# Chunked attention and a gated feed-forward layer on one core: steps of blocks 2 to 4 moved, the weights' sign by a sloped ReLU, and more products on nothing in block 0's attention

## The chip, the cores and the metric

The kernel runs on one core of one Trainium2 chip. The core has five engines that run side by side and each take their instructions in order: TensorE (PE in the profile; its weight loads are PEld), VectorE (DVE), ScalarE (ACT), GpSimd (POOL) and SyncE (SP), which here issues the transfers. The metric is the device time of one execution in microseconds (us).

## The reference

Queries, keys and values have 8 batches, 8 heads, 576 positions and 64 columns. Attention works within chunks of 64 positions, and its output goes through a feed-forward layer with a gate:

```python
scores = scale * np.matmul(q_c, k_c.transpose(0, 1, 2, 4, 3))
scores = scores - np.max(scores, axis=-1, keepdims=True)
attn = np.exp(scores)
attn = attn / (np.sum(attn, axis=-1, keepdims=True) + 1e-09)
out = np.matmul(attn, v_c)
...
h = x @ w_in                        # x: 4608 x 512, w_in: 512 x 2048
relu6 = np.clip(h + 3.0, 0.0, 6.0)
g = h * relu6 / 6.0
return (g @ w_out).astype(np.float32)   # w_out: 2048 x 512
```

All is in 32-bit floats.

## The kernel before

**Tiles and blocks.** The 4608 rows of x are nine blocks of 512 tokens. A block's attention has two halves, dp = 0 and 1, of four heads each; (2, 1) below is the second half of block 2. The 2048 columns between the two products are 16 tiles, ft = 0 to 15. Each factor of a product is split into a high part that the array takes exactly and a low rest, and a product is three matmuls (`passes`, L221 to L223: high by high, high by low, low by high).

**Attention** (L128 to L209) goes in steps: `load_qk` and `load_v` (transfers, one tile each, so a load waits for the use before), `scores` (64 small matmuls, L154, into the PSUM tile "two"), `soft` steps 0 to 3 (row maximum m, L161; subtraction and exponential, L164 and L165; sums z with the reciprocal, L168 to L170; normalization, L172), `transpose` (eight on TensorE, L183, and ScalarE's copy back over e, L185), `values` (64 small matmuls, L194, and ScalarE's copy of the result as x, L203 or L200; for blocks 0 to 2 VectorE makes the low rest of x, L206, at the end of the slot). After block 0 there is one PSUM tile "two" for all of it.

**The weights** arrive as 64-bit floats, and `convert` (L100 to L116) makes the split 32-bit ones: ScalarE copies the high word with a scale (L106), VectorE shifts it left by three bits (L107), which pushes the sign out, and puts the sign back by an AND with the word and an OR (L108). Then ScalarE scales the low word (L110), VectorE adds it (L111), ScalarE makes the high part (L115) and VectorE the low one (L116). `convert` runs once for each of the 16 tiles, four of them for block 0's first products, the others behind `issue_after` bounds on block 1's softmax.

**The start.** Block 0's attention stands ahead of all products (L291 to L307). `warm_up(n)` issues n matmuls of the identity by itself into a tile that nobody reads, "products on nothing"; `WARM2` holds how many of them stand at five places: after both scores, after both softmaxes (36), none, and in each half's turn between transposes and values (6) and after the values (4).

**Slots.** Blocks 0, 1 and 2 are computed directly, in the order of `SEGMENTS`: block 0 with tiles 0 to 3, block 1 with 0 to 15, block 0 with 4 to 15, block 2 with 0 to 15. Each tile has two slots: in the even one `mm1` makes 12 matmuls into h, followed by the gate (ScalarE L233, VectorE L234, ScalarE L235, and VectorE L236 at the slot's end); in the odd one `mm2` makes 12 matmuls of an earlier tile's g (LAG tiles behind) into four accumulators, which are evicted after a segment's last tile (L259 to L266). At the end of each slot the steps that `plan` has for it are issued, by rank and then in the order in which they were put there. Ahead of slot 30 (`SUMS`) a scheduler of the framework may change the order on the engines; from there on the text's order stands (`manual_schedule`). So what is issued first on a queue keeps back what is behind it. The attention of blocks 2 to 4 is put at the slots 30, 38, 52, 60, 68 and 76 for (2,0), (2,1), (3,0), (4,0), (4,1) and (3,1), with the offsets of the list `later`; all six are even.

**Units.** Blocks 3 to 8 are later multiplied in pairs by seven products in place of eight, and need sums of weights. `prepare(m, p)` (L328 to L356) makes them in 16 units, which start at the slots 30, 33, 36, 40, 43, 46, 50, 53, 57, 60, 63, 67, 70, 73, 77 and 80. A unit has three steps in three slots in a row, of rank 20 (behind all attention steps of the slot): first three transfers of plain weights to DRAM (L333) and two adds of high and low parts on VectorE (L337); second four sums on VectorE (L347) and ScalarE's copy of their high parts into the tile hl (L350); third VectorE's low parts into hl (L352) and four transfers of hl to DRAM (L355). The tiles a and hl have one buffer each, so L350 waits until the unit before has sent its hl.

**After.** At slot 86 (`FREE`) the memory of the weights and units is given to the paired products: `fetch` loads the sums from DRAM, and `x_operands` makes the operands of blocks 3 and 4 (L372, L373) in the slots behind 86. Block 2's products end at slot 96 and the pending ones behind it; from there the paired products run to the end, with the attention of blocks 5 to 8 among them.

Of the kernel before, what the change touches and what calls it, by code (L numbers as in the profile page):

```python
# [8 lines left out]
F32 = mybir.dt.float32  # L9
# [4 lines left out]
AF = mybir.ActivationFunctionType  # L14
ALU = mybir.AluOpType
# [15 lines left out]
NFP = NFT // 2  # L31
# [2 lines left out]
SLOTS = 7 * NFP  # L34
HALF = [slice(0, CH), slice(CH, P)]
WARM = 11
WARM2 = (0, 36, 0, 6, 4)
LAG = 2


# [1 line left out]
def tile_kernel(ctx: ExitStack, tc: tile.TileContext, qk_in, v_in, weights, out):  # L42
    nc = tc.nc
    PE, ACT, DVE, POOL = nc.tensor, nc.scalar, nc.vector, nc.gpsimd
# [31 lines left out]
    def warm_up(n, a=some, b=some):  # L76
        if not n:
            return
        idle = ps_h.tile([P, NT], F32, name="h")[:, :b.shape[-1]]
        for _ in range(n):  # L80
            PE.matmul(idle, lhsT=a[:, :P], rhs=b, start=True, stop=True)
# [7 lines left out]
    words, w, w_h, w_l = {}, {}, {}, {}  # L89
    loaded = converted = 0  # L90

    def load_to(ft):
        nonlocal loaded
        while loaded < min(ft, NFT):
            t = w_tile(loaded, I32).rearrange("p l m t -> p (l m t)")
            nc.sync.dma_start(out=t.rearrange("p (m t) -> p m t", m=2), in_=weights[loaded].bitcast(I32).rearrange("m p t -> p m t"))
            words[loaded] = t.rearrange("p (n t) -> p n t", t=2)
            loaded += 1

    def convert(ft):  # L100

        u = wsc.tile([P, 1024], I32, name="u")
        r = wsc.tile([P, 1024], I32, name="r")
        lo, hi = words[ft][:, :, 0], words[ft][:, :, 1]

        ACT.activation(out=u.bitcast(F32), in_=hi.bitcast(F32), func=AF.Copy, scale=2.0 ** -112)  # L106
        DVE.tensor_scalar(out=u, in0=u, scalar1=3, scalar2=None, op0=ALU.logical_shift_left)  # L107
        DVE.scalar_tensor_tensor(out=u, in0=hi, scalar=-2 ** 31, in1=u, op0=ALU.bitwise_and, op1=ALU.bitwise_or)  # L108

        ACT.activation(out=r, in_=lo.bitcast(U32), func=AF.Copy, scale=2.0 ** -29)  # L110
        DVE.tensor_tensor(out=u, in0=u, in1=r, op=ALU.add)  # L111
        a = u.bitcast(F32).rearrange("p (m t) -> p m t", m=2)
        w[ft] = w_tile(ft, F32R)
        w_h[ft], w_l[ft] = w[ft][:, 0], w[ft][:, 1]
        ACT.copy(out=w_h[ft], in_=a)  # L115
        DVE.tensor_tensor(out=w_l[ft], in0=a, in1=w_h[ft].bitcast(F32), op=ALU.subtract)  # L116

    def convert_to(ft):
        nonlocal converted
        load_to(ft + 3)  # L120
        while converted < min(ft, NFT):
            convert(converted)
            converted += 1

    def two_banks(p):
        return p.tile([P, 2, NT], F32, name="two")
# [88 lines left out]
    def finish():  # L215
        while low:
            low.pop(0)()
# [56 lines left out]
    def moe_slots(n, ft, *seg):  # L274

        g = mm1(n, ft)
        yield
        pending.append((n, ft, g, *seg))
        if len(pending) > LAG:
            mm2(*pending.pop(0))  # L280
        yield
# [9 lines left out]
    with tc.tile_pool(name="ps_b", bufs=2, space=bass.MemoryType.PSUM) as ps_b:  # L291
        both = [Attention(0, dp, lambda: two_banks(ps_b)) for dp in range(NDP)]
        both[0].load()
        both[1].load(xp.tile([P, 2, NB, 2 * CH], F32, name="x"), gp.tile([P, 2, NB // 2, 2 * CH], F32, name="g"))
        load_to(4)
        for a in both:
            a.scores()
        warm_up(WARM2[0])
        both[0].softmax()
        both[1].softmax(gp.tile([P, 2, NB, CH], F32, name="g"))  # L300
        warm_up(WARM2[1])
        for a in both:
            a.transpose()
            warm_up(WARM2[3])
            a.values()
            finish()
            warm_up(WARM2[4])  # L307
    ps_o = pool("ps_o", 4, space=bass.MemoryType.PSUM)
    convert_to(2)

# [6 lines left out]
    def kept(m, p, i):  # L317

        if m:
            return stream_b[i, p // 4][:, p % 4]  # L320
        k = ORDER_A.index(i)
        return stream_a[p, k // 4][:, k % 4]

    def quarter(m, row, col):

        return (col, row) if m else (row, col)

    def prepare(m, p):  # L328
        cols = lambda k: slice(256 * k, 256 * k + 256)
        for i, row, col in ((1, 0, 0), (2, 0, 1), (4, 1, 1)):  # L330
            f, k = quarter(m, row, col)
            to = kept(m, p, i).rearrange("p (l t) -> p l t", l=2)
            nc.sync.dma_start(out=to, in_=w[p + NFP * f][:, :, m, cols(k)].bitcast(F32))  # L333
        a = sp.tile([P, 2, 512], F32, name="a")
        for f in range(2):
            h, l = [w[p + NFP * f][:, k, m].bitcast(F32) for k in range(2)]
            DVE.tensor_tensor(out=a[:, f], in0=h, in1=l, op=ALU.add)  # L337
        yield

        def q(row, col):  # L340
            f, k = quarter(m, row, col)
            return a[:, f, cols(k)]


        for to, x, y, op in ((q(1, 1), q(1, 0), q(1, 1), ALU.add), (q(1, 0), q(0, 0), q(1, 0), ALU.subtract),
                             (q(0, 0), q(1, 1), q(0, 0), ALU.subtract), (q(0, 1), q(0, 1), q(0, 0), ALU.subtract)):
            DVE.tensor_tensor(out=to, in0=x, in1=y, op=op)  # L347
        hl = sp.tile([P, 2, 2, 2, 256], F32R, name="hl")
        s = a.rearrange("p f (k t) -> p f k t", k=2)
        ACT.copy(out=hl[:, :, :, 0], in_=s)  # L350
        yield
        DVE.tensor_tensor(out=hl[:, :, :, 1], in0=s, in1=hl[:, :, :, 0].bitcast(F32), op=ALU.subtract)  # L352
        for i, row, col in ((5, 1, 1), (7, 1, 0), (6, 0, 0), (3, 0, 1)):
            f, k = quarter(m, row, col)
            nc.sync.dma_start(out=kept(m, p, i), in_=hl[:, f, k].rearrange("p l t -> p (l t)").bitcast(F32))  # L355
        yield  # L356


# [21 lines left out]
    def x_operands(s, eng):  # L380
# [6 lines left out]
        for i in ORDER_A:  # L387
# [6 lines left out]
            elif i == 6:  # L394
# [6 lines left out]

    plan = {}
    early = [(0, "load_qk"), (1, "load_v"), (2, "scores"), (2, "softmax"), (7, "transpose"), (10, "values")]
    later = [(-2, "load_qk"), (3, "load_v"), (3, "scores"), (4, "soft", 0), (4, "soft", 1), (5, "soft", 2), (5, "soft", 3),
             (8, "transpose"), (9, "values")]

    def put(n, dp, at, steps, stretch=1.0):
        a = Attention(n, dp)
# [7 lines left out]
    SUMS = first[1] + 22  # L416
    FREE = first[3] + 2 * (NFP + LAG + 1)
    for (n, dp), at in zip(((2, 0), (2, 1), (3, 0), (4, 0), (4, 1), (3, 1)), (30, 38, 52, 60, 68, 76)):
        put(n, dp, at, later)
    for u in range(2 * NFP):  # L420
        for k in range(3):
            plan.setdefault(SUMS + u * (FREE - 2 - SUMS) // (2 * NFP) + k, []).append((20, lambda: next(prep)))
    prep = (step for p in range(NFP) for m in range(2) for step in prepare(m, p))
    slot = 0
    sp = made = None
    order = ExitStack()

    for i, (n, lo, hi) in enumerate(SEGMENTS):
        last = all(m != n for m, *_ in SEGMENTS[i + 1:])
        for ft in range(lo, hi):  # L430
            if i == 0:
                convert_to(min(ft + 2, 4))
            elif slot < SUMS:

                with tc.issue_after(second.done.ins):
                    convert_to(5)
                with tc.issue_after(second.last.ins):
                    convert_to(min(6 + 2 * ft, NFT))
            elif slot == SUMS:
                scratch.close()  # L440
                sums = ExitStack()
                sp = sums.enter_context(tc.tile_pool(name="sp", bufs=1, side="right"))
                op = sums.enter_context(tc.tile_pool(name="op", bufs=4, side="right"))
                order.enter_context(tc.manual_schedule())
            for _ in moe_slots(n, ft, ft == lo, ft == hi - 1, not last):
                for _, f in sorted(plan.pop(slot, []), key=lambda s: s[0]):
                    f()
                finish()
                slot += 1
                if slot == FREE:  # L450
                    assert next(prep, None) is None
                    sums.close()
                    op = None
                    start.close()
                    upper.close()
                    xop_pool = pool("xop", 8, side="right")
                    wsp = pool("wsp", 3, side="right")
                    for _ in range(3):
                        fetch()
                    made = x_operands(0, DVE)  # L460
                elif slot > FREE:
                    next(made, None)
# [197 lines left out]
```

## Time and profile before

| | us |
|---|---|
| median of 3 runs (854.91 to 855.72) | 855.14 |
| the profiled execution | 855.06 |
| its span, first to last instruction | 853.1 |
| TensorE busy | 814.5 |
| VectorE busy | 635.8 |
| ScalarE busy | 369.1 |
| GpSimd busy | 132.0 |

How to read it: busy times are sums over the span and overlap each other. A timeline row gives start, length, engine, line, operation, what is written from what, and in brackets how long the engine had been idle and what ended it; several instructions alike in a row are one row with their count. A row of a windows table gives a stretch, its length, the busy time of TensorE, its weight loads, VectorE, ScalarE and GpSimd with the number of instructions, then the clock granted to TensorE (1.00 is full), the busy share of the transfer engines and GB/s. Matmuls overlap, so the length of one is more than the distance to the next.

### The profile page before, as it was taken

How to read it: one execution, taken by the hardware profiler on the slowest of the kernel's cores; microseconds unless marked ns; L12 is line 12 of the kernel's file. 1: busy time of each engine (PE TensorE's matmuls, PEld its weight loads, DVE VectorE, ACT ScalarE, POOL GpSimd, SP SyncE). 2: the span in 40 equal slices, each digit the busy share in tenths (PEclk: the TensorE clock that was granted, in tenths of full speed). 3: DMA queues.
4: the chain of work that ended last, by engine and by line, in shares of the span. 5: the costliest groups of instructions: out<-in, count | busy, mean ns of one | idle time of the engine just before them, and what ended most of it. 6: DMA issues, size and time to landing. Idle time of an engine off the chain costs nothing.

```text
span 853.1 us, 13690 instructions
## 1 busy us (share of the span) xinstructions
PE 814.5 (95%) x5683; PEld 658.7 (77%) x5683; DVE 635.8 (75%) x768; ACT 369.1 (43%) x455; POOL 132.0 (15%) x77
## 2 busy tenths in 40 slices
PE   7889999789998999999999999999999999999998
PEld 5766878568776777878878888788788887887886
DVE  5978997585866776487699946876899466669951
ACT  4747763243334334334455443344554333336330
POOL 0000000000001000022227002222370022326200
PEclk9898999899999999999999999999999999999999
DMA  9893003856768745166655576666554765555563
GB/s 365 315 360 120 13 0 112 247 184 214 220 187 296 237 160 196 60 232 226 244 189 191 229 254 228 233 214 245 204 192 167 234 226 178 207 186 197 197 212 134
DMA packets 50014, 172.86 MB, mean 203 GB/s; under 512 B 4640, under 2 KB 16928, under 8 KB 39200
## 3 DMA queue, kind: packets, MB, share of 16 engines
q1 hardware_dynamic: 49952, 171.99, 58.0%
q8 instruction: 45, 0.74, 0.3%
q14 instruction: 17, 0.14, 0.1%
HBM read 133.17 MB, written 38.80 MB: 202 GB/s over the span
## 4 chain that ended last, share of the span: by engine, by line
PE 67%; DVE 22%; ACT 5%; issue 3%; DMA 2%; POOL 0%; SPq 0%; ACTq 0%; DVEq 0%
PE acc L221 14%; PE acc L223 14%; PE acc L222 14%; PE h L221 7%; PE h L222 7%; PE h L223 7%; PE two L194 2%; DVE xop L373 2%; DVE m L161 2%; DVE r L234 2%; DVE z L168 1%; DMA w<-w_in_out 1%; DVE a L347 1%; DVE e L164 1%; DVE g L496 1%
## 5 line engine op out<-in xcount | busy, mean ns | idle before, releaser
L221 PE MATMUL acc<-xop,ws 128*128 128x512 f32 x528 | 208.6, 396 | 4.4 <-DVE u L484 4.4
L222 PE MATMUL acc<-xop,ws 128*128 128x512 f32 x528 | 205.8, 390 | 0.0
L223 PE MATMUL acc<-xop,ws 128*128 128x512 f32 x528 | 205.4, 390 | 0.0
L221 PEld LDWEIGHTS acc<-xop,ws 128*128 128x128 f32 x528 | 99.1, 188 | 27.6 <-DVE u L484 6.8
L373 DVE TENSOR_TENSOR xop<-g,xop 128x1024 fp32r<-128x1024 f32 x72 | 103.4, 1468 | 21.5 <-ACT xop L372 21.5
L223 PEld LDWEIGHTS acc<-xop,ws 128*128 128x128 f32 x528 | 99.1, 188 | 20.9
L222 PEld LDWEIGHTS acc<-xop,ws 128*128 128x128 f32 x528 | 99.2, 188 | 19.8
L372 ACT CAST xop<-g 128x1024 fp32r<-128x1024 f32 x72 | 74.4, 1051 | 78.9 <-PE acc L223 51.3
L504 POOL TENSOR_TENSOR g<-g 128x512 f32<-128x512 f32 x24 | 34.8, 1449 | 307.3 <-DVE g L496 307.3
L221 PE MATMUL h<-x,w 128*128 128x512 f32 x192 | 80.0, 419 | 2.1 <-ACT x L203 1.2
L222 PE MATMUL h<-x,w 128*128 128x512 f32 x192 | 78.4, 409 | 0.0
L223 PE MATMUL h<-x,w 128*128 128x512 f32 x192 | 77.8, 405 | 0.0
L222 PE MATMUL acc<-g,w 128*128 128x512 f32 x192 | 75.5, 393 | 0.3 <-DVE g L236 0.3
L221 PE MATMUL acc<-g,w 128*128 128x512 f32 x192 | 75.4, 397 | 0.1
L223 PE MATMUL acc<-g,w 128*128 128x512 f32 x192 | 75.4, 393 | 0.0
L234 DVE SCALAR_TENSOR_TENSOR r<-r,h 128x512 f32<-128x512 f32 x48 | 32.8, 683 | 50.7 <-ACT r L233 50.7
L495 ACT ACTIVATE r<-acc,half 128x512 f32<-128x512 f32 x72 | 48.5, 685 | 26.3 <-DVE acc L484 25.4
L495 ACT ACTIVATE r<-h,half 128x512 f32<-128x512 f32 x24 | 16.5, 687 | 95.0 <-DVE h L484 95.0
L222 PE MATMUL h<-xop,ws 128*128 128x512 f32 x144 | 56.2, 390 | 0.2 <-DVE xop L373 0.2
L221 PE MATMUL h<-xop,ws 128*128 128x512 f32 x144 | 56.3, 391 | 0.0
L223 PE MATMUL h<-xop,ws 128*128 128x512 f32 x144 | 56.1, 389 | 0.0
L496 DVE SCALAR_TENSOR_TENSOR g<-r,acc 128x512 f32<-128x512 f32 x72 | 48.6, 683 | 7.0 <-ACT r L495 6.7
(93 smaller groups left out, 1270.5 us busy)
## 6 DMA issues: line engine op xcount, KB each, us to landing
ws<-b SPq DMA_DIRECT2D x42, 1024.0 KB, 4.8
ws<-a SPq DMA_DIRECT2D x24, 1024.0 KB, 4.9
ws<-a SPq DMA_DIRECT2D x24, 768.0 KB, 4.3
qk<-qk_in SPq DMA_DIRECT2D x17, 1024.0 KB, 6.6
w<-w_in_out SPq DMA_DIRECT2D x16, 1024.0 KB, 13.4
v<-v_in SPq DMA_DIRECT2D x17, 512.0 KB, 5.1
a<-hl SPq DMA_DIRECT2D x32, 256.0 KB, 3.4
b<-hl SPq DMA_DIRECT2D x32, 256.0 KB, 3.4
```

The costliest lines, as they stand in the source:

```text
L161: DVE.tensor_reduce(out=self.m, in_=flat(self.s), axis=AX.X, op=ALU.max)
L164: DVE.tensor_tensor(out=flat(self.e), in0=flat(self.s), in1=wide(self.m), op=ALU.subtract)
L194: PE.matmul(po[o, s, a, i, :], lhsT=self.v[rows, a, i, o], rhs=self.aT[rows, a, i, o], start=True, stop=True)
L221: PE.matmul(ps, lhsT=a_h, rhs=b_h, start=first, stop=False, skip_group_check=more)
L222: PE.matmul(ps, lhsT=a_h, rhs=b_l, start=False, stop=False, skip_group_check=more)
L223: PE.matmul(ps, lhsT=a_l, rhs=b_h, start=False, stop=last, skip_group_check=more)
L234: DVE.scalar_tensor_tensor(out=r, in0=r, scalar=1.0, in1=h, op0=ALU.min, op1=ALU.mult)
L372: ACT.copy(out=t[:, :, 0], in_=src)
L373: DVE.tensor_tensor(out=t[:, :, 1], in0=src, in1=t[:, :, 0].bitcast(F32), op=ALU.subtract)
L495: return (lambda: ACT.activation(out=r, in_=ps, func=AF.Relu, bias=half, scale=1.0 / 6.0), lambda: DVE.scalar_tensor_tensor(out=out, in0=r ...
L496: lambda: DVE.scalar_tensor_tensor(out=out, in0=r, scalar=1.0, in1=ps, op0=ALU.min, op1=ALU.mult))
L504: sub = lambda o, x, y: lambda: POOL.tensor_tensor(out=o, in0=x, in1=y, op=ALU.subtract)
```

## The change

Three things change. (1) `WARM2` has 46, 12 and 18 for 36, 6 and 4, and the last count is issued behind the first half only: 88 products on nothing instead of 56. (2) In `convert` the first step is ScalarE's sloped ReLU: it scales by 2^-112, and negative inputs by 2^32 more, which sets a bit of the exponent that the shift by three then moves into the sign's place; VectorE's L108 is gone. (3) The steps in `later` are moved, most of them by one slot ahead, with `load_v` behind the first softmax steps; a unit of `prepare` has four steps in four slots (the two adds; the four sums; the copy into hl; the low parts and all seven transfers, those of hl first and those of plain weights behind them), and each unit is a generator of its own, so that one unit's last step can share a slot with the next one's first.

```diff
-WARM2 = (0, 36, 0, 6, 4)
+WARM2 = (0, 46, 0, 12, 18)
...
-        ACT.activation(out=u.bitcast(F32), in_=hi.bitcast(F32), func=AF.Copy, scale=2.0 ** -112)
+        ACT.activation(out=u.bitcast(F32), in_=hi.bitcast(F32), func=AF.Prelu, scale=2.0 ** -112, alpha=2.0 ** 32)
         DVE.tensor_scalar(out=u, in0=u, scalar1=3, scalar2=None, op0=ALU.logical_shift_left)
-        DVE.scalar_tensor_tensor(out=u, in0=hi, scalar=-2 ** 31, in1=u, op0=ALU.bitwise_and, op1=ALU.bitwise_or)
...
             finish()
-            warm_up(WARM2[4])
+            if a is both[0]:
+                warm_up(WARM2[4])
...
     def prepare(m, p):
         cols = lambda k: slice(256 * k, 256 * k + 256)
-        for i, row, col in ((1, 0, 0), (2, 0, 1), (4, 1, 1)):
-            f, k = quarter(m, row, col)
-            to = kept(m, p, i).rearrange("p (l t) -> p l t", l=2)
-            nc.sync.dma_start(out=to, in_=w[p + NFP * f][:, :, m, cols(k)].bitcast(F32))
         a = sp.tile([P, 2, 512], F32, name="a")
...
             DVE.tensor_tensor(out=to, in0=x, in1=y, op=op)
+        yield
         hl = sp.tile([P, 2, 2, 2, 256], F32R, name="hl")
...
             nc.sync.dma_start(out=kept(m, p, i), in_=hl[:, f, k].rearrange("p l t -> p (l t)").bitcast(F32))
+        for i, row, col in ((1, 0, 0), (2, 0, 1), (4, 1, 1)):
+            f, k = quarter(m, row, col)
+            to = kept(m, p, i).rearrange("p (l t) -> p l t", l=2)
+            nc.sync.dma_start(out=to, in_=w[p + NFP * f][:, :, m, cols(k)].bitcast(F32))
         yield
...
-    later = [(-2, "load_qk"), (3, "load_v"), (3, "scores"), (4, "soft", 0), (4, "soft", 1), (5, "soft", 2), (5, "soft", 3),
-             (8, "transpose"), (9, "values")]
+    later = [(-3, "load_qk"), (2, "scores"), (3, "soft", 0), (3, "soft", 1), (3, "load_v"), (4, "soft", 2), (4, "soft", 3),
+             (7, "transpose"), (8, "values")]
...
     for u in range(2 * NFP):
-        for k in range(3):
-            plan.setdefault(SUMS + u * (FREE - 2 - SUMS) // (2 * NFP) + k, []).append((20, lambda: next(prep)))
-    prep = (step for p in range(NFP) for m in range(2) for step in prepare(m, p))
+        unit = prepare(u % 2, u // 2)
+        for k in range(4):
+            plan.setdefault(SUMS + u * (FREE - 2 - SUMS) // (2 * NFP) + k, []).append((20, lambda unit=unit: next(unit)))
```

More of the change, by code (lines that the diff above doesn't have):

```diff
@@ L450, in tile_kernel @@
                 if slot == FREE:
-                    assert next(prep, None) is None
                     sums.close()
```

## The prediction

> **What bounds the kernel now.** I read the page first, then the windows of each stage, then the waits of TensorE by place, and only there the timelines.
>
> ```profile
> span 853.1 us, 13690 instructions
> ...
> PE 814.5 (95%) x5683; PEld 658.7 (77%) x5683; DVE 635.8 (75%) x768; ACT 369.1 (43%) x455; POOL 132.0 (15%) x77
> ```
>
> TensorE is busy for 95% of the span, so the time is TensorE's work plus the places where it idles or runs at a lower clock. The profiled execution took 855.06 us, 1.96 us more than its span, and stands 0.08 us under the median of 855.14 us; I sum against 855.06. The windows by stage (stretch, its length, then busy time of TensorE, weight loads, VectorE, ScalarE, GpSimd, then the granted clock) show where it idles:
>
> ```profile
> 0.00:23.30 23.30, 16.64 (x276) 11.67 (x276) 14.60 (x18) 11.20 (x12) 1.16 (x7) 1.00 0.94 369
> ...
> 58.80:71.10 12.30, 7.98 (x81) 6.13 (x82) 9.68 (x11) 5.51 (x6) 0.00 (x0) 0.59 0.94 375
> 71.10:125.00 53.90, 52.97 (x225) 41.74 (x225) 52.60 (x60) 41.03 (x49) 0.00 (x0) 1.00 0.02 7
> 125.00:322.20 197.20, 179.96 (x1486) 145.27 (x1485) 138.97 (x214) 72.61 (x95) 3.11 (x2) 0.97 0.65 205
> ```
>
> From 71 to 125 us VectorE is full (52.60 of 53.90), but TensorE too: work taken off VectorE there is worth under 1 us. From 125 to 322.2 us (slots 30 to 85) TensorE idles 197.20 - 179.96 = 17.2 us with VectorE at 70%. It is all in six places, the values of blocks 2, 3 and 4 waiting for ScalarE's copy of the transposed weights (L185); the bracket is the idle time:
>
> ```profile
> 159.95 1.98 PE L194 MATMUL two<-e,v 64*64 64x64 f32 x64 [6.35 <-ACT e L185]
> ...
> 190.25 1.69 PE L194 MATMUL two<-e,v 64*64 64x64 f32 x64 [2.72 <-ACT e L185]
> ...
> 235.31 1.16 PE L194 MATMUL two<-e,v 64*64 64x64 f32 x64 [1.63 <-ACT e L185]
> ...
> 264.14 0.29 PE L194 MATMUL two<-e,v 64*64 64x64 f32 x4 [2.69 <-ACT e L185]
> ...
> 293.31 0.29 PE L194 MATMUL two<-e,v 64*64 64x64 f32 x4 [1.72 <-ACT e L185]
> ...
> 320.99 0.33 PE L194 MATMUL two<-e,v 64*64 64x64 f32 x5 [2.03 <-ACT e L185]
> ```
>
> Their sum is 17.1 us. Behind the three longest the clock falls:
>
> ```profile
> 158.40:163.40 5.00, 3.45 (x68) 3.05 (x69) 2.03 (x3) 2.51 (x3) 0.00 (x0) 0.50 0.86 277
> 190.20:195.00 4.80, 4.75 (x73) 4.05 (x74) 3.08 (x6) 2.06 (x3) 0.00 (x0) 0.64 0.96 280
> 265.00:269.40 4.40, 4.40 (x33) 3.46 (x24) 1.23 (x1) 1.38 (x2) 0.00 (x0) 0.61 1.07 390
> ```
>
> Busy time times the missing clock: 3.45 x 0.50 + 4.75 x 0.36 + 4.40 x 0.39 = 5.1 us. So 22.2 us are to be had there. Behind the gaps of 1.63, 1.72 and 2.03 us I take the clock as kept, since the first row after the 1.63 has the fast 1.16.
>
> **The changed steps of blocks 2 to 4.** This is the largest term. First why the values wait. For the first of the six:
>
> ```profile
> 149.37 1.79 SPq L355 DMA_DIRECT2D b<-hl  x4
> ...
> 155.98 1.04 ACT L350 CAST hl<-a 128x1024 fp32r<-128x1024 f32 x1 [5.39 <-DMA b<-hl]
> ...
> 158.89 1.01 ACT L185 COPY e<-two 128x1024 f32<-128x1024 f32 x1
> ```
>
> There is one hl buffer. The next unit's copy into it (L350) stands on ScalarE's queue for 5.39 us until the four writes have left, 155.98 - 149.37 = 6.6 us after their first issue, and L185 stands behind it. The second shows the other cause:
>
> ```profile
> 173.85 1.22 DVE L161 TENSOR_REDUCE m<-two 128x16 f32<-128x1024 f32 x1
> ...
> 177.97 1.28 DVE L264 COPY o<-acc 128x512 f32<-128x512 f32 x2
> ...
> 179.17 1.21 DVE L168 TENSOR_REDUCE z<-e 128x16 f32<-128x1024 f32 x1
> 180.91 1.23 DVE L172 TENSOR_TENSOR e<-e,z 128x1024 f32<-128x1024 f32 x1
> 182.06 1.28 DVE L337 TENSOR_TENSOR a<-w 128x512 f32<-128x512 f32 x2
> 183.26 0.68 DVE L234 SCALAR_TENSOR_TENSOR r<-r,h 128x512 f32<-128x512 f32 x1
> ...
> 183.70 1.04 PE L183 MATMUL two<-ident,e 128*128 128x128 f32 x8
> 183.86 1.80 DVE L347 TENSOR_TENSOR a<-a 128x256 f32<-128x256 f32 x4
> ...
> 186.82 1.23 DVE L352 TENSOR_TENSOR hl<-a,hl 128x1024 fp32r<-128x1024 f32 x1 [0.56 <-ACT hl L350]
> ...
> 188.67 0.62 ACT L235 CAST g<-r 128x512 fp32r<-128x512 f32 x1 [1.31 <-DVE r L234]
> 189.20 1.00 ACT L185 COPY e<-two 128x1024 f32<-128x1024 f32 x1
> ```
>
> The transposes were done at 184.74, but the copy ran at 189.20. The transposes sit in slot 46, an even slot, so that slot's own gate (relu, L234, then L235) is ahead of L185 on ScalarE, and L234 is behind a VectorE backlog. The change puts the transposes into odd slots (at+7), with no gate of their own, and the softmax a slot earlier.
>
> A slot takes 2.75 us, five of them lying between these two rows:
>
> ```profile
> 136.08 0.50 PE L221 MATMUL h<-x,w 128*128 128x512 f32 x1
> ...
> 149.82 1.03 PE L183 MATMUL two<-ident,e 128*128 128x128 f32 x8
> ```
>
> Worked by hand for (2,1), zero at the end of its scores in slot 40. VectorE: the rest of slot 40 (gate, two adds L337, g) to 2.3; m and the subtraction, 1.2 each, to 4.7; L347 to 6.5; slot 42's gate, released by its matmuls at 5.5, to 7.2; the three z steps, 1.7, to 8.9; L172 to 10.1; g 10.8; L264 12.1; L352 13.3; L337 14.6; slot 44's gate 15.3. ScalarE: L235 to 15.9, L185 to 16.9. TensorE: slots 41 to 45 to 13.75, transposes to 14.8, slot 46 to 17.5, then the values. L185 is 0.6 us early: no wait, where there were 2.72. The same count with the before order gives 3.4 us, so such a count is good to about 0.7.
>
> The others, counted alike, with the units' new slots (copy L350 at start + 2: 35, 38, 42, 45, 48, 52, 55, 59, 62, 65, 69, 72, 75, 79, 82; L352 and the writes one later): (2,0), transposes in slot 37, is early by 1.6; (3,0), slot 59, by 0.4; (4,0), slot 67, by 0.7; (4,1), slot 75, by 0.7. In (2,0) the copy held 5.39 us now falls into slot 35, where its input comes at 11.6 and the writes of slot 33 (L352 ends at 3.6 to 4.6) are out by about 11. One stays: (3,1) transposes in slot 83, and the last unit's copy is in slot 82, two slots behind writes that are issued at 12.8. They land between
>
> ```profile
> a<-hl SPq DMA_DIRECT2D x32, 256.0 KB, 3.4
> ```
>
> 3.4 us after the last of four issues (12.8 + 1.4 + 3.4 = 17.6) and the 6.6 above (19.4); the gate of slot 82 ends at 17.9 on ScalarE. Copy and L185 take 2.05, so the values wait to 20 to 21.5: 2.5 to 4 us. I take 3, and 1.7 us of lower clock behind it. For the thin margins I take 1 us in all. Sum: -17.1 + 3 + 1 - 5.1 + 1.7 = -16.5 us.
>
> What else moves: the three writes of weights (L333) go from the first step of a unit to its last, behind the hl writes on SyncE, so the hl buffer is free no later for them. load_qk moves to the slot at+3 before, load_v behind the softmax; SyncE may hold them behind a late L352 by some 5 us, against 5 slots (13.7 us) until the values. The last unit's writes end about two slots later, about slot 87, when the first operands for block 3 reuse that memory; covered, since the products that need them start at slot 96. If not covered, 1 to 3 us. The wait of L352 for L350 is now a slot apart from it: cost nothing, it even spares 0.56.
>
> **Block 0 and the weights' sign.** Each of 16 conversions loses one VectorE step:
>
> ```profile
> L108 DVE SCALAR_TENSOR_TENSOR u<-w,u 128x1024 int32<-128x1024 int32 x16 | 19.5, 1219 | 0.0
> ```
>
> Four belong to the weights of block 0's products; the other twelve wait for block 1's softmax (issue_after) and stand beside the full TensorE of 71 to 125 us. The sloped ReLU in place of a copy (L106) is not in this trace. It is an ACTIVATE over the same elements; I take the same time, and bound it below by nothing gained.
>
> ```profile
> 10.62 4.00 PE L81 MATMUL h<-ident 128*128 128x256 bf16 x35
> ...
> 18.71 1.16 PE L194 MATMUL two<-e,v 64*64 64x64 f32 x64 [0.94 <-ACT e L185]
> ...
> 24.66 1.98 PE L194 MATMUL two<-g 64*64 64x64 f32 x64 [0.72 <-ACT g L185]
> ...
> 23.30:30.80 7.50, 6.78 (x79) 5.26 (x77) 7.50 (x8) 5.37 (x6) 0.00 (x0) 0.54 0.82 328
> ```
>
> Products on nothing: 36 + 6 + 4 + 6 + 4 = 56 become 46 + 12 + 18 + 12 = 88, so 32 more, 32 x 4.00/35 = 3.7 us of TensorE. The 0 to 23.3 us window leaves it 6.7 us idle, and they fall into the waits for L172 and L185 there, so I cost them at nothing; on the path they would cost 3.7. With the waits filled the clock should hold: the second half's values take 1.16 for 1.98, and all of the stretch from 23.3 to 30.8 us has at most 6.78 x 0.46 = 3.1 us to give back. The rest of x comes through those values, and VectorE has fewer L108 ahead of it. I take 2.5. Then the second stall:
>
> ```profile
> 60.79 1.80 PE L183 MATMUL two<-ident,e 128*128 128x128 f32 x8 [2.01 <-DVE e L172]
> ...
> 66.86 0.79 PE L221 MATMUL h<-x,w 128*128 128x512 f32 x1 [1.18 <-ACT x L203]
> ```
>
> TensorE has no products of block 0 left and waits for block 1's second half, whose chain of VectorE steps starts from the first's. It moves with TensorE's start (2.5) up to four L108 (4.9); I take 3.5 in all for the product at 66.86, and 0.5 for the small waits until 125 us. If the gap also shrinks enough to keep the clock, 7.98 x 0.41 = 3.3 more. So -4, from 0 to -9.
>
> Sum: 855.06 - 16.5 - 4 = 834.6; I say 834.5.
>
> [...] My clock terms say that a gap of 2.69 us is followed by a clock of 0.61. [...]
>
> **The rivals.** *The margins are eaten.* The early copies have 0.4 to 1.6 us, and If each of the six keeps a gap like the three small ones (mean 1.8, sum 10.8, no lower clock), the steps bring 17.1 - 10.8 + 5.1 = 11.4: 839.7 with block 0's 4 us, 843.7 without. For: L185 ran 4.5 us behind its transposes above, for VectorE's backlog alone. Against: the hand count, in which that backlog is passed by one slot.
>
> *The dummies and the order do nothing.* The order ahead of slot 30 is not the text's (56 dummies stand as 16, 35 and 5 in the trace). If the new ones land where no wait is, block 0 gains nothing and pays 3.7: 834.5 + 4 + 3.7 = 842.2. Against: the 35 above end before the transposes that wait behind them.
>
> *The sloped ReLU switches tables* (the slower side). The only load now is
>
> ```profile
> L71 ACT ACT_TABLE_LOAD x1 | 1.3, 1283 | 0.7 <-PEq L653 0.7
> ```
>
> though Exp, Relu and Copy alternate. If the new function shares a table with none of them, each conversion takes two loads, 2.57 us of ScalarE. The first four are on the way to the first products: +10.3. The other twelve, 30.8, meet 53.90 - 41.03 = 12.9 us of free ScalarE: +17.9. That gives 834.5 + 28 = 862.5. It decides from about 1.1 us a load. Against: three functions in one table. [...]
>
> **How the numbers follow.** 0.2% (1.7 us) is about what a measurement of this kernel can tell from no change. Forecast 0.60 (826 to 840, by the bounds of its terms: block 0 from 0 to -9, the slot 83 wait and the margins 2 us either way); margins eaten 0.20 (839 to 844); dummies on the path 0.10 (842.2); tables 0.05 (862.5); the rest, the moved steps meeting a wait that I don't see, 0.05, split over same and slower. The range 826 to 844 leaves out the last two and the ends. Faster 0.90, same 0.03, slower 0.07.
>
> **What would show it.** Right: no L194 wait over 1 us between slots 30 and 82, one of 2.5 to 4 us near the end of that stage with L350 waiting for hl's writes ahead of it, a clock of 1.00 from 23 to 31 us, L108 gone, one table load. Wrong: waits at L194 that stay, a new wait at L183 for L172, idle time before L106 on ScalarE, or a first operand copy (L372) held by the weights' writes.

## The result and the profile after

The changed kernel takes 831.77 us (median of 4 runs, 831.42 to 832.11), beside 855.38 us for the kernel before on the same chip (median of 4, 854.91 to 855.72). The ratio is 0.9724, 95% interval 0.9707 to 0.9741: 23.6 us faster. The profiled execution took 832.07 us. In the changed kernel the lines sit one or two off: L185 is L186, L194 is L195, L106 is L108, L350 is L349, L355 is L354, and the gate's L233 and L235 are L234 and L236.

Its page (span; busy time and share of the engines):

```profile
span 830.1 us, 13748 instructions
...
PE 809.1 (97%) x5715; PEld 656.8 (79%) x5715; DVE 620.2 (75%) x752; ACT 366.6 (44%) x455; POOL 132.4 (16%) x77
```

VectorE's busy time fell by 15.6 us and kept its share of 75%, TensorE went from 95% to 97%. The windows by stage, of the changed kernel (stretch, length, busy time of TensorE, weight loads, VectorE, ScalarE, GpSimd, then the clock):

```profile
23.30:30.80 7.50, 4.91 (x81) 3.48 (x78) 6.90 (x8) 7.50 (x9) 0.00 (x0) 1.00 1.01 406
...
67.50:120.50 53.00, 53.00 (x225) 42.86 (x225) 43.62 (x52) 41.87 (x51) 0.00 (x0) 0.98 0.03 11
120.50:295.50 175.00, 172.10 (x1474) 139.88 (x1473) 136.30 (x209) 70.19 (x94) 3.45 (x2) 1.00 0.69 223
295.50:830.10 534.60, 526.27 (x3259) 430.08 (x3258) 391.33 (x434) 215.87 (x269) 127.75 (x68) 1.00 0.58 204
```

From 120.5 to 295.5 us, the stage of blocks 2 to 4, TensorE idles 2.90 us in all; in the kernel before, this stage had 17.2. The 2.90 are one wait, at the values of (3,1). The changed kernel's timeline there:

```profile
285.71 2.56 SPq L354 DMA_DIRECT2D a<-hl  x4
...
289.93 0.62 ACT L236 CAST g<-r 128x512 fp32r<-128x512 f32 x1 [4.78 <-DVE r L235]
...
291.66 1.04 ACT L349 CAST hl<-a 128x1024 fp32r<-128x1024 f32 x1 [1.11 <-DMA a<-hl]
292.61 1.00 ACT L186 COPY e<-two 128x1024 f32<-128x1024 f32 x1
...
293.67 1.16 PE L195 MATMUL two<-e,v 64*64 64x64 f32 x64 [2.90 <-ACT e L186]
```

The last unit's copy (L349) waits 1.11 us for the writes of hl, and the copy that the values need (L186) stands behind it. The copy itself takes about 1 us more; the rest is the gate ahead of both (L236), which had waited for VectorE. The gate of slot 30 starts at 122.36 us for 127.00 before, that of slot 86 at 302.21 for 325.20, and from there to the end both traces have 527.9 us. So the start gave 4.6 us, the moved steps 18.4, and the rest of the kernel nothing.

The rival by tables fell at once. In the changed kernel's groups by line (busy, mean ns of one, idle before):

```profile
L108 ACT ACTIVATE u<-w 128x1024 f32<-128x1024 f32 x16 | 18.2, 1141 | 4.1 <-DMA w<-w_in_out 4.1
...
L71 ACT ACT_TABLE_LOAD x1 | 1.3, 1283 | 0.7 <-PEq L655 0.7
```

One load, and the sloped ReLU takes 1.14 us, as long as the copy had (1.15).

### The profile page after: what moved, and what is told of

The parts are those of the page before. It is cut to its first block, busy times and chain, and to the rows that moved or that the text cites. A ratio compares the mean times of both kernels' runs of the same rounds, so it can differ in the third digit from the quotient of the medians.

```text
span 830.1 us, 13748 instructions
## 1 busy us (share of the span) xinstructions
PE 809.1 (97%) x5715; PEld 656.8 (79%) x5715; DVE 620.2 (75%) x752; ACT 366.6 (44%) x455; POOL 132.4 (16%) x77
## 4 chain that ended last, share of the span: by engine, by line
PE 79%; DVE 10%; ACT 5%; issue 2%; DMA 2%; SPq 0%; POOL 0%; ACTq 0%; DVEq 0%
PE acc L222 17%; PE acc L223 16%; PE acc L224 16%; PE h L223 8%; PE h L222 8%; PE h L224 8%; DVE xop L376 2%; PE two L195 2%; PE two L155 1%; DMA w<-w_in_out 1%; PE two L184 1%; DVE g L498 1%; DVE u L486 1%; ACT r L497 1%; DVE z L169 1%
## 5 line engine op out<-in xcount | busy, mean ns | idle before, releaser
L222 PE MATMUL h<-x,w 128*128 128x512 f32 x192 | 77.2, 403 | 3.1 <-ACT x L204 3.1
L222 PE MATMUL acc<-g,w 128*128 128x512 f32 x192 | 77.4, 403 | 0.0
L223 PE MATMUL h<-x,w 128*128 128x512 f32 x192 | 77.1, 401 | 0.0
L224 PE MATMUL h<-x,w 128*128 128x512 f32 x192 | 76.3, 398 | 0.0
L223 PE MATMUL acc<-g,w 128*128 128x512 f32 x192 | 76.1, 396 | 0.0
L224 PE MATMUL acc<-g,w 128*128 128x512 f32 x192 | 76.0, 396 | 0.0
L235 DVE SCALAR_TENSOR_TENSOR r<-r,h 128x512 f32<-128x512 f32 x48 | 32.8, 684 | 45.1 <-ACT r L234 45.0
L497 ACT ACTIVATE r<-h,half 128x512 f32<-128x512 f32 x24 | 16.5, 687 | 94.4 <-DVE h L486 94.4
L234 ACT ACTIVATE r<-h,half 128x512 f32<-128x512 f32 x48 | 32.8, 684 | 50.9 <-PE h L224 50.8
```

Source lines behind the costliest of these rows:

```text
L222: PE.matmul(ps, lhsT=a_h, rhs=b_h, start=first, stop=False, skip_group_check=more)
L223: PE.matmul(ps, lhsT=a_h, rhs=b_l, start=False, stop=False, skip_group_check=more)
L224: PE.matmul(ps, lhsT=a_l, rhs=b_h, start=False, stop=last, skip_group_check=more)
L234: ACT.activation(out=r, in_=h, func=AF.Relu, bias=half, scale=1.0 / 6.0)
L235: DVE.scalar_tensor_tensor(out=r, in0=r, scalar=1.0, in1=h, op0=ALU.min, op1=ALU.mult)
L497: return (lambda: ACT.activation(out=r, in_=ps, func=AF.Relu, bias=half, scale=1.0 / 6.0), lambda: DVE.scalar_tensor_tensor(out=out, in0=r ...
```

## The experiments

All medians stand beside the kernel before on the same chip, 855.1 to 855.4 us.

**The three parts alone.** The moved steps (`later`, the four-step units):

```diff
-    later = [(-2, "load_qk"), (3, "load_v"), (3, "scores"), (4, "soft", 0), (4, "soft", 1), (5, "soft", 2), (5, "soft", 3),
-             (8, "transpose"), (9, "values")]
+    later = [(-3, "load_qk"), (2, "scores"), (3, "soft", 0), (3, "soft", 1), (3, "load_v"), (4, "soft", 2), (4, "soft", 3),
+             (7, "transpose"), (8, "values")]
...
-        for k in range(3):
+        for k in range(4):
```

> The kernel before with the moved steps alone (the list of offsets and the four-step units). If the stage of blocks 2 to 4 stands by itself, it gives all that the traces show from slot 30 on, 23.0 - 4.6 = 18.4 us: 837.0 us, with one wait of about 2.9 us at the values of (3,1) and none over 1 us at the other five. The rival, that the stage runs clean only because VectorE enters it without the backlog of the sign steps, leaves one or two of the first waits standing: 841 us or more.

Measured: 834.57 us, ratio 0.9765 (0.9747 to 0.9783). In its trace slot 30 comes when it did before, and the steps give 20.5 us by slot 86, more than the 18.4 inside the whole change. The one wait left is 2.33 us, and no clock is lost behind it (1.00 from 297 to 303 us); in the changed kernel it is 2.90 us, and the clock is:

```profile
293.00:299.00 6.00, 5.33 (x76) 4.39 (x77) 2.34 (x3) 2.74 (x4) 0.00 (x0) 0.72 0.74 247
```

5.33 x 0.28 = 1.5 us. (Why one wait costs clock and the other doesn't is taken up at the end.) Ahead of that wait the two traces run alike: by the gates' starts, counted from slot 30, both are 12.5 us ahead of the kernel before at slot 48 and 19.5 at slot 80. The stage needs nothing from the start; the rival falls.

The sloped ReLU:

```diff
-        ACT.activation(out=u.bitcast(F32), in_=hi.bitcast(F32), func=AF.Copy, scale=2.0 ** -112)
+        ACT.activation(out=u.bitcast(F32), in_=hi.bitcast(F32), func=AF.Prelu, scale=2.0 ** -112, alpha=2.0 ** 32)
...
-        DVE.scalar_tensor_tensor(out=u, in0=hi, scalar=-2 ** 31, in1=u, op0=ALU.bitwise_and, op1=ALU.bitwise_or)
```

> The kernel before with the sloped ReLU alone, L108 gone. After the trace: the first products did not come earlier, the gain of the start appears at slots 2 to 6, where VectorE makes the other weights, so the 16 steps less are what brings it: 3.5 to 4.5 us, about 851.4. The rival is the prediction as it stands: 1 us from these steps, 2.5 from the clock, so about 854.4 here. Both expect one table load and the function's time within 3% of the copy's 1.15 us.

Measured: 848.35 us, 0.9917 (0.9902 to 0.9932), 6.9 us: more than either theory, and on the side of the one that gives the start's gain to VectorE's steps.

The products on nothing:

```diff
-WARM2 = (0, 36, 0, 6, 4)
+WARM2 = (0, 46, 0, 12, 18)
```

> The kernel before with 88 instead of 56 products on nothing alone. By the prediction the clock stays at 1.00 from 23 to 31 us and this brings 2.5 us: 852.9. The rival after the trace: the clock does stay, but ScalarE is full there and hands the second half of x over no earlier, so the first gate (the relu of slot 0, at 32.0 us before) moves by less than 0.5 us and the time stays: 855.4.

Measured: 855.35 us, 1.0000 (0.9990 to 1.0011). Nothing. Two windows of its trace, then its ScalarE and TensorE rows (here the lines have the old numbers):

```profile
17.53:20.94 3.41, 3.41 (x45) 2.43 (x47) 3.36 (x6) 3.28 (x5) 0.00 (x0) 0.50 1.04 413
...
23.30:30.80 7.50, 6.61 (x96) 4.80 (x95) 7.50 (x8) 5.55 (x7) 0.00 (x0) 1.00 1.02 407
```

```profile
17.55 2.56 PE L81 MATMUL h<-ident 128*128 128x256 bf16 x11
20.04 1.55 PE L194 MATMUL two<-e,v 64*64 64x64 f32 x64
...
22.62 1.21 ACT L110 ACTIVATE r<-w 128x1024 int32<-128x1024 uint32 x1
23.73 1.16 ACT L106 ACTIVATE u<-w 128x1024 f32<-128x1024 f32 x1
24.80 0.99 ACT L185 COPY g<-two 128x1024 f32<-128x1024 f32 x1
...
25.84 1.16 PE L194 MATMUL two<-g 64*64 64x64 f32 x64
```

From 23.3 us on the clock is 1.00 where it was 0.54, and the second half's values take 1.16 us instead of 1.98. But the clock is at half earlier, from 17.53 to 20.94 us. There 11 of the products stand ahead of the first half's values, which start at 20.04 us for 18.71, though the copy that they need is done at 18.81. The second half's copy stands behind two steps of the weights and comes at 24.80 us instead of 23.57, VectorE is busy for all 7.50 us, and the first gate starts at 33.30 us for 32.03: later by 1.3, where under 0.5 was expected. So what the clock gives is lost ahead of it. The expectation laid the loss on ScalarE's being full; here it isn't (5.55 of 7.50). How the loss splits between the early half clock, the products on the path and the order is not shown, and this is the trace of one execution.

Both changes of the start:

> The kernel before with both changes of the start, without the moved steps. If the two stages add up, this has the 4.6 us that the traces show at slot 30: 850.8 us; the rest of the change is then the steps' 18.4. If the stages depend on each other, this and the steps alone sum to more or less than 23.6 by over 2 us.

Measured: 849.53 us, 0.9931 (0.9919 to 0.9943), 5.7 us. That is less than the sign alone, though the two intervals overlap; by the traces, slot 30 is 5.3 us ahead of the kernel before here, and 7.0 with the sign alone. With the steps' 20.7 it sums to 26.4 where the whole change has 23.6, so by the line that was drawn the stages are not independent. By the traces, 2.2 of the 2.8 us lie at the one wait left (20.5 against 18.4 us of the steps), and most of that in the clock behind it (1.00 with the steps alone, 0.72 in the changed kernel), which by the last section the length of a wait alone does not settle. So it isn't shown that the stages need each other.

**The two halves of the moved steps.** The offsets alone:

> The kernel before with the new offsets of the attention steps alone, units in three steps as before. Theory: the waits come from what stands ahead of L185 on ScalarE (the gate of an even slot, or a copy held by the hl writes) and the new offsets alone pass both in five of six places: 839 us, one wait of 1 to 3 us left at (3,1), clock kept elsewhere. Rival: the units' order (four steps, writes of plain weights last) is what frees the hl buffer in time; then the offsets alone keep the 6.35 us wait or one like it, 848 us or more.

Measured: 841.03 us, 0.9829 (0.9812 to 0.9845). The wait left is a bigger one and at another place, (4,1):

```profile
276.29 1.04 ACT L350 CAST hl<-a 128x1024 fp32r<-128x1024 f32 x1 [4.09 <-DMA a<-hl]
...
278.30 0.94 PE L194 MATMUL two<-e,v 64*64 64x64 f32 x32 [4.08 <-ACT e L185]
```

The units alone:

> The kernel before with the four-step units alone, offsets as before. Theory: the copy into hl moves behind L185 at (2,0) (slot 38, later rank), so the 6.35 us wait and the clock behind it go (about 7.9 us), while the five waits behind an even slot's gate stay at 1.5 to 3 us: about 847.5. Rival: the units' order is the main thing: below 842.

Measured: 857.22 us, 1.0022 (1.0013 to 1.0031). Both expectations miss: the units alone make it slower. The 6.35 us wait did shrink, to 2.19, but others grew: at (2,1) from 2.72 to 3.53, at (3,1) from 2.03 to 2.58, and at (4,1) from 1.72 to:

```profile
288.54 1.04 ACT L347 CAST hl<-a 128x1024 fp32r<-128x1024 f32 x1 [3.47 <-DMA a<-hl]
...
292.51 1.24 PE L194 MATMUL two<-e,v 64*64 64x64 f32 x36 [4.36 <-ACT e L185]
```

I had counted which copies leave the slot ahead of a transposition, and not which enter it. By the list of slots, the largest wait of each run has one pattern: the copy stands in the slot right ahead of the transposes, and the writes of the unit before are two slots ahead of the copy. These are slots 37 and 35 for transposes in 38 (the kernel before), 74 and 72 for 75 (offsets alone), 75 and 73 for 76 (units alone), 82 and 80 for 83 (the whole change, its only such place). Units alone have it at (2,1) too (45 and 43 for 46, the 3.53 us). Offsets alone also have it a second time, at (2,1) (44 and 42 for 45), but there the copy waited 1.14 us for VectorE's sums and not for the writes, and the values waited only 0.81 us. So each half alone leaves two such places and together they leave one, and the pattern tells where a copy can be held, not that it will be.

**An even slot.** The changed kernel with transposes at +8 and values at +9:

> The changed kernel with transposes and values one slot later again (at+8 and at+9, the slots of before), the softmax left a slot ahead. Theory by the count of the queues: the slot's own gate is again ahead of L185, but VectorE's backlog has been passed by then, so waits stay under 1 us at (2,0) and (2,1), and the wait at (3,1) falls, since one more slot lies behind the held copy: within 3 us of the changed kernel, 829 to 833. Rival, that the odd slot as such is what counts: waits of 1.5 to 2.7 us in five places again, 840 us or more.

Measured: 839.61 us, 0.9816 (0.9802 to 0.9831), 7.8 us over the changed kernel. Six waits of 1.1 to 3.8 us are back. At (2,1), which I had counted early:

```profile
173.17 1.05 ACT L349 CAST hl<-a 128x1024 fp32r<-128x1024 f32 x1 [2.99 <-DMA b<-hl]
...
175.56 0.62 ACT L236 CAST g<-r 128x512 fp32r<-128x512 f32 x1 [0.75 <-DVE r L235]
176.08 1.01 ACT L186 COPY e<-two 128x1024 f32<-128x1024 f32 x1
177.14 1.04 PE L195 MATMUL two<-e,v 64*64 64x64 f32 x56 [2.01 <-ACT e L186]
```

The chain is held copy, relu, VectorE, the slot's own gate, L186. My count had left out the held copy. Copies held for 1.8 to 3.0 us stand ahead at (2,1), (3,0), (4,1) and (3,1); at (2,0) and (4,0) the slot's own gate is alone, and the waits are 1.12 and 1.25 us. So the odd slots are worth about 8 of the 18 us, by the gate and the held copies together, and the theory that it was VectorE's backlog alone falls; the rival's sizes (1.5 to 2.7) are nearer.

**The first wait by itself.** The kernel before, with one unit moved:

```diff
-            plan.setdefault(SUMS + u * (FREE - 2 - SUMS) // (2 * NFP) + k, []).append((20, lambda: next(prep)))
+            plan.setdefault(SUMS + u * (FREE - 2 - SUMS) // (2 * NFP) + k + (u == 2), []).append((20, lambda: next(prep)))
```

> The kernel before with the third unit alone put one slot later (37 for 36), so that its copy into hl is issued behind L185 of (2,0) in slot 38. Theory: the copy held by the hl writes makes the first wait; 6.35 us becomes about 0.7, the clock behind it stays, the other five waits are as before: 7.2 us less, 848.2. Rival, VectorE's backlog alone makes that wait too: it stays over 2.5 us, and the time is 852 or more.

Measured: 849.88 us, 0.9938 (0.9921 to 0.9955), 5.2 us for the 7.2. The wait fell nearly as expected:

```profile
154.69 1.02 PE L194 MATMUL two<-e,v 64*64 64x64 f32 x53 [1.13 <-ACT e L185]
```

The trace is 6.8 us ahead at slot 40 and gives back 3.4 by slots 48 and 62, behind waits that are hardly longer than before (2.78 and 1.90 us for 2.72 and 1.63). It is the clock that differs there; of this run

```profile
183.90:189.00 5.10, 5.06 (x71) 4.27 (x72) 3.06 (x6) 2.06 (x2) 0.00 (x0) 0.50 0.90 263
230.50:235.50 5.00, 4.95 (x74) 4.13 (x75) 1.85 (x5) 0.64 (x1) 0.00 (x0) 0.66 1.05 264
```

and of the kernel before

```profile
190.20:195.20 5.00, 4.95 (x74) 4.21 (x75) 3.08 (x6) 2.06 (x3) 0.00 (x0) 0.66 0.92 269
235.30:240.30 5.00, 4.99 (x81) 4.28 (x82) 1.81 (x5) 2.21 (x3) 0.00 (x0) 1.00 1.05 264
```

**The last wait.** The changed kernel with `k + (u == 15)`:

> The changed kernel with the last unit alone one slot later (81 for 80), so that its copy into hl is issued in slot 83 behind L185 of (3,1). Theory: the one wait left (2.9 us, and 5.33 x 0.28 = 1.5 us of clock behind it) goes whole: 827.4 us. Rival: the writes of that unit now end a slot later and hold the first operands of block 3 at slot 87, which gives back 1 to 3 us; then 829 to 831.

Measured: 826.85 us, 0.9663 (0.9650 to 0.9676), 4.9 us under the changed kernel. The copy is still held, but behind L186, where it costs nothing:

```profile
288.46 1.01 ACT L186 COPY e<-two 128x1024 f32<-128x1024 f32 x1
...
290.55 1.16 PE L195 MATMUL two<-e,v 64*64 64x64 f32 x64
291.50 1.05 ACT L349 CAST hl<-a 128x1024 fp32r<-128x1024 f32 x1 [2.04 <-DMA a<-hl]
```

The later writes held no operands.

**A wait made on purpose.** The changed kernel with `k - (u == 8)`:

> The changed kernel with the ninth unit alone one slot earlier (56 for 57). Its copy then stands in slot 58, right ahead of the transposes of (3,0) in slot 59, two slots behind the writes of the unit before (slot 56): the pattern of the one wait left. Theory, that this pattern makes the wait: a new one of 2.3 to 4 us at the values of (3,0), which had none, with up to 1.7 us of clock behind it: 834.3 to 837.5. Rival, that the wait at (3,1) comes from the end of the stage: no new wait, 831.8.

Measured: 833.58 us, 0.9743 (0.9730 to 0.9756), 1.8 us over the changed kernel. The two intervals overlap, but the trace loses 1.9 us against the changed kernel's between slots 48 and 62, where the wait stands. It is at the expected place, and smaller:

```profile
213.00 0.62 ACT L236 CAST g<-r 128x512 fp32r<-128x512 f32 x1 [4.85 <-DVE r L235]
213.55 1.04 ACT L349 CAST hl<-a 128x1024 fp32r<-128x1024 f32 x1
...
214.50 1.01 ACT L186 COPY e<-two 128x1024 f32<-128x1024 f32 x1
...
215.56 1.16 PE L195 MATMUL two<-e,v 64*64 64x64 f32 x64 [1.87 <-ACT e L186]
```

The copy went straight behind the gate; the writes were out. So this wait is not one behind a held copy: it is the copy's own 1.04 us and the gate's wait for VectorE ahead of it. In other runs a hold came on top, until the writes had left (1.11 us in the changed kernel, 4.09 with the offsets alone).

**Without the additional products.** The changed kernel with `WARM2 = (0, 36, 0, 6, 4)` and its `warm_up` behind both halves:

> The changed kernel with the 56 products on nothing of before. Theory: the 32 more are not needed for the clock once VectorE hands the second half's weights over a step earlier, and with them the order ahead of slot 30 puts two steps of the weights ahead of ScalarE's copy for the second half's values; without them the start gains 1 to 2 us: about 830.5. The sum of the single runs (steps 20.7, sign 6.9) would give 827.7. Rival, the prediction's: without them the clock falls at 23 us and 2.5 us are lost: 834.3.

Measured: 827.81 us, 0.9679 (0.9666 to 0.9692), 4.0 us under the changed kernel. By the traces 2.2 us are in the start. The other 2.2 are at the wait of (3,1), 2.28 us here, behind which the clock stays (that this part comes from the products is not shown; see the last section):

```profile
290.00:296.00 6.00, 5.20 (x82) 4.45 (x83) 2.47 (x3) 2.87 (x4) 0.00 (x0) 1.00 0.61 211
```

The changed kernel's own rows show where the start loses its part; ScalarE:

```profile
22.39 1.15 ACT L108 ACTIVATE u<-w 128x1024 f32<-128x1024 f32 x1
23.45 1.12 ACT L111 ACTIVATE r<-w 128x1024 int32<-128x1024 uint32 x1
24.48 0.98 ACT L186 COPY g<-two 128x1024 f32<-128x1024 f32 x1
```

In the kernel with the sign alone, which has the 56 products, that copy is ahead of both steps:

```profile
22.39 1.01 ACT L184 COPY g<-two 128x1024 f32<-128x1024 f32 x1
...
23.46 1.16 PE L193 MATMUL two<-g 64*64 64x64 f32 x64 [0.41 <-ACT g L184]
```

So it is in every trace with the sign: the copy is ahead of both steps in the three with 56 products, and behind both in the five with 88.

**Both mends.** The 56 products and the last unit one slot later:

> The changed kernel with the 56 products on nothing of before and the last unit one slot later. If both theories hold and the places are independent, the two gains add: 831.8 - 4.4 - 1.3 = 826.1 us. Rival: less than the better one of the two alone.

Measured: 825.02 us, 0.9645 (0.9632 to 0.9658): 30.4 us under the kernel before and 6.8 under the changed one. It is the fastest of all, and the stage of blocks 2 to 4 has no idle time left:

```profile
118.00:292.00 174.00, 174.00 (x1484) 141.45 (x1483) 135.85 (x209) 70.44 (x94) 3.45 (x2) 1.00 0.69 224
```

## Why the prediction was right, and where it wasn't

The forecast of 834.5 us lies 2.7 over the measured time, inside the range, and its largest term carried it.

*The moved steps, -16.5 forecast, -18.4 found.* The idle time went from 17.1 to 2.9 us and the lost clock from 5.1 to 1.5, 17.8 together; the remaining 0.6 is not broken down. The hand count placed the one wait (slot 83, 2.5 to 4 us, taken as 3; 2.90 found) and its cause, L349 held by hl's writes. The 1 us for thin margins was not needed: counted early by 1.6, 0.6, 0.4, 0.7 and 0.7 us, the other five copies end 1.5, 1.1, 0.9, 0.8 and 1.4 us before their values start. The two causes were named rightly. The held copy is shown by moving one unit away (the third in the kernel before, 5.2 us; the last in the changed kernel, 4.9). The even slot's gate is shown at the two places of the even-slot run where no held copy stands (1.12 and 1.25 us); the whole 7.8 us of that run hold both causes. The count's stated error of 0.7 us did not cover what it left out: at (2,1) of the even-slot run under 1 us was expected, and with a held copy ahead it came to 2.01. That the clock falls behind the one wait (1.7 us forecast, 1.5 found) is in part luck, as the last section shows.

*The start, -4 forecast, -4.6 found, and the step that failed.* The product at 66.86 us was to come 3.5 earlier and comes 3.6 earlier:

```profile
63.27 0.80 PE L222 MATMUL h<-x,w 128*128 128x512 f32 x1 [2.21 <-ACT x L204]
```

That the sum fits is luck: two errors cancel. "With the waits filled the clock should hold ... I take 2.5" is the step that failed. In the profiled execution the clock did hold, and the first gate still started at 32.33 us for 32.03 before. And the products are neither needed for the clock nor sure to keep it. First the run with the sign alone and 56 products, then the run with the last unit moved, which has the changed kernel's start:

```profile
23.30:30.80 7.50, 6.51 (x84) 4.59 (x85) 7.36 (x8) 7.50 (x9) 0.00 (x0) 1.00 0.82 326
...
23.30:30.80 7.50, 5.78 (x80) 4.36 (x79) 6.92 (x7) 7.50 (x9) 0.00 (x0) 0.77 1.01 405
```

The additional products bring 0.0 us alone, and they cost beside the sign: slot 30 is ahead of the kernel before by 4.6 to 5.4 us in the five traces with both, and by 6.9 to 7.0 in the three with the sign and 56 products. The 16 steps off VectorE bring 6.9. In the run with the sign alone, block 1's first product shows 5.3 of them:

```profile
61.57 0.50 PE L220 MATMUL h<-x,w 128*128 128x512 f32 x1 [1.77 <-ACT x L202]
```

I had given these steps 1 us beyond the clock, though VectorE was full (7.50 of 7.50) in the very row that I had quoted for the clock. That the products could be costed at nothing, since they fall into waits, failed as well: alone, they held the first half's values by 1.2 us (20.04 for 18.81), and beside the sign the order ahead of slot 30 was another with them, and put two ScalarE steps ahead of the copy that the values need. Why that order comes out so was not tried.

*The rivals.* Margins eaten: no. Dummies on the path: in part, they cost (not the 3.7 us that it named) and didn't bring, but the sign paid for it. Tables: no. From 71 to 125 us VectorE's full queue was indeed worth little: it fell from 52.60 of 53.90 to 43.62 of 53.00 busy, and TensorE went from 52.97 to 53.00.

*The clock behind gaps.* The prediction took a lower clock behind a gap of about 3 us from the rows of the kernel before, 0.61 behind 2.69 us among them. The 2.90 us gap cost 1.5 us of clock (0.72 from 293 to 299 us), as the rows had it; the last section has shorter ones that cost it too, 1.90 and 2.19 us, and others, up to 2.58 us, that did not.

## What to carry to other kernels

Where engines take their work strictly in order, list for each wait what stands ahead of the instruction that ends it, and count the slots of every step that can be held, those that a move brings in as well as those that it takes away. Half of such a change can be worth nothing, or less, while the whole is worth much. Before covering a gap for the clock's sake, see whether the work behind it waits for another engine: here the cover brought nothing (855.35 us, ratio 1.0000).

## What the runs showed that I had not expected

The length of a gap alone does not settle whether the clock falls behind it. It stayed at 1.00 behind 2.28 us (without the additional products, to 296 us), behind 2.33 (with the steps alone, to 303) and behind 2.58 (at (3,1) with the units alone, from 323 to 329). It fell behind 2.90 (0.72 in the changed kernel), and in the kernel before behind 2.72 (0.66) and 2.69 (0.61). But it fell behind 1.90 us too (0.66 in the run with one unit moved, above), and with the units alone behind 2.19:

```profile
156.00:161.00 5.00, 3.83 (x71) 3.18 (x72) 3.14 (x3) 3.08 (x4) 0.00 (x0) 0.75 0.46 161
```

In the two traces of the kernels before and after, within the span, the clock was at half for 3.4, 6.8 or 10.2 us at a time, and its changes lie whole multiples of 3.41 us apart. Three of these stretches, in the kernel before:

```profile
60.96:71.20 10.24, 7.91 (x81) 6.00 (x80) 7.52 (x8) 5.61 (x6) 0.00 (x0) 0.50 0.91 364
156.53:163.36 6.83, 3.41 (x68) 3.01 (x69) 2.74 (x4) 3.63 (x5) 0.00 (x0) 0.50 0.89 301
190.67:194.08 3.41, 3.41 (x57) 2.91 (x50) 2.43 (x5) 1.38 (x2) 0.00 (x0) 0.50 1.06 310
```

Two waits can be set side by side on that scale: 1.90 us in the run with one unit moved in the kernel before (228.65 to 230.55) and 2.33 us in the run with the steps alone (295.41 to 297.75). Cut into stretches of 3.41 us along each trace's own changes, first the one, then the other:

```profile
227.81:231.22 3.41, 1.51 (x48) 1.05 (x50) 3.38 (x7) 1.53 (x2) 0.00 (x0) 1.00 0.63 207
231.22:234.64 3.42, 3.42 (x42) 2.75 (x31) 1.16 (x3) 0.00 (x0) 0.00 (x0) 0.50 1.12 255
...
293.22:296.63 3.41, 2.19 (x10) 1.49 (x8) 1.98 (x4) 1.51 (x2) 0.00 (x0) 1.00 1.05 314
296.63:300.04 3.41, 2.29 (x69) 2.05 (x70) 2.26 (x3) 2.66 (x5) 0.00 (x0) 1.00 0.39 137
300.04:303.45 3.41, 3.41 (x16) 2.82 (x16) 0.34 (x1) 0.53 (x1) 0.00 (x0) 1.00 0.82 277
```

The shorter wait lies within one stretch, in which TensorE is busy for 1.51 of 3.41 us, and 3.42 us at half clock follow. The longer one is split over two stretches, busy for 2.19 and 2.29, and the clock stays at 1.00. So between these two it was not the longer wait that cost the clock, but the one that fell into a single stretch. That this is the cause, and that other waits of 2 to 3 us go by it, is not shown: each trace shows one such placement.
